# Transposed keys through DRAM in five transfers, with a new order of work, in a gated linear attention and PReLU network kernel

## The chip, the cores and the metric

The kernel runs on one core of a Trainium2 chip. The metric is the time of one execution on the device, in microseconds; the smaller the better. The profile comes from one execution of its own, and its times are counted from that execution's first instruction.

## The reference

Two blocks follow each other. The first is a recurrence over 768 positions with a state of 48 x 48 for each of 4 batches x 8 heads; the second is a network over all 3072 tokens with a PReLU between two matrices.

```python
f = 1.0 / (1.0 + np.exp(-f_logit))
for t in range(S):                      # S = 768
    state = f[:, :, t, :, None] * state + np.einsum('bhd,bhe->bhde', k[:, :, t], v[:, :, t])
    y[:, :, t] = np.einsum('bhd,bhde->bhe', q[:, :, t], state)
x = y.transpose(0, 2, 1, 3).reshape(B * S, H * D)     # 3072 x 384
h = x @ w_in                                          # 384 x 2048
g = np.maximum(h, 0.0) + alpha * np.minimum(h, 0.0)
return g @ w_out                                      # 2048 x 384
```

Everything is float32.

## The kernel before

**Steps.** The positions are cut into six chunks of 128 and the four batches into two pairs. One step handles one chunk of one pair, so there are 12 steps, numbered 0 to 11, alternating between the pairs. Steps 0 and 1 (`opening`) have no state to carry in; steps 2 to 11 are the "usual" ones (`usual`, L427). The recurrence of a step is turned into matrix products: scores inside the chunk (`raw`, `qu`, `off`), the part that comes from the carried state, and the new state. The tokens that come out go through the network (`network`, L812) while the next steps' recurrence is under way, so TensorE works on the network of step n-1 and the recurrence of step n at once.

**An order written out by hand.** The text `ORDER_WORDS` (L41) is a list of 1186 words. A word such as `5K` names part `K` of step 5, and the kernel issues the parts in the order of the list. For TensorE (PE), VectorE (DVE) and ScalarE (ACT) that is the order in which they execute. GpSimd (POOL) and SyncE (SP), which issue transfers, get their order from the framework's own scheduling. Words that the prediction names: `e` loads q, k, the gates f and v of a step; `f` is the sigmoid and copies, `F`, `g`, `G`, `h`, `i`, `l` the elementwise work on keys and queries; `k` the transposition of the keys on VectorE; `K` their way to where the matmuls can use them; `d` the state increments on TensorE; `D` and `M` add these to the state; `r`, `u`, `o` are score matmuls, `R`, `U`, `O` and `A` put their results into the score matrix A; `y` is the output product, `Y` and `X` its way to the network. In the network (`N`), `a` is a product with `w_in` into one bank, `r` and `c` the PReLU, `b` the third pass of a product taken in three passes (four of the eight parts, from step 3 on), `p` a block product with `w_out` (tiles `pa` to `pf`), `m`, `u`, `v`, `w` sums of blocks of the gated values (L881), `Y` and `Z` accumulating transfers issued by GpSimd. `I` and `J` are matmuls without a use that keep TensorE running at the start.

**The keys.** The state increment of a step is keys transposed times values. In a usual step, `fifth` (L465, word `k`) lets VectorE transpose the tile `ks` in blocks of 32 x 32 into `x["kt"]`; that tile is the buffer into which the gates were loaded (tag `f`, one buffer, L311). After that the blocks stand on the wrong partitions. `keys` (L469, word `K`) moves them with 16 transfers on SyncE's queue, from SBUF to SBUF: for each of four groups of 32 source partitions and each of four groups of 32 target partitions one transfer of 32 partitions x 8 runs of 32 or 16 floats (128 or 64 bytes), into the tile `ksn`. `increments` (L531, word `d`) then runs 64 small matmuls that read `ksn` and the values `vs`, into the tile `pd` (L540). As `f` has one buffer, the load of the next step's gates (L313, GpSimd's queue) can't start until the transfers have read `kt`.

**Other transfers on SyncE's queue** are the stores of the result (`store`, L764, tile `o`) and the way of the step's output tokens through DRAM (`given`, L497: two transfers to DRAM, L504, and one back, L506).

Of the kernel before, what the change touches and what calls it, by code (L numbers as in the profile page):

```python
# [8 lines left out]
F32 = mybir.dt.float32  # L9
# [37 lines left out]
0Np4 Y3 0Np5 1Y1 2G 1X W0 W1 W2 0Np6 W3 W4 W5 0Np7 1Na0 0No0 2h 1M 0No1 2i 1Na3 1Nr0 1Na1 Y4 Y5 2p 1Na2 1Nr1 3e 2q
Y6 1Na4 1Nr2 2k 2r0 2u0 2l W6 1Nc0 1Nr3 1Nc1 2K 1Nm0 1Nr4 1Nc2 2t W7 1Na5 1Nc3 1Nm1 1Nc4 1Na6 1Nr5 2R0 2r1 2U0 1Nr6
1Na7 Z3 2R1 2A0 1Nc6 2u1 1Nr7 1Nc5 2o Z4 1Np0 2U1 2O 1Nc7 2A1 2d 1Nk 1Np1 2D 3f 3F 2y0 2y1 2M 2Y0 2Y1 1Np2 1Np3 2X
1Nu0 3g 1Nu1 1Nv0 1Np4 1Nd 1Nv1 1Nw0 1Ng 3G 1Nw1 1Ne 1Nj 1Nh 1Np5 1Np6 3h 1Nf 1Nl 1Ni 3p 1Ns1 2Na2 2Na0 3i 1NL 1Ns0  # L50
2Nr0 2Na1 3l 2Nr1 4e 2Na3 3q 2Nr2 2Nc0 3r0 3u0 2Nr3 3k 2Nc1 3R0 2Nm0 3K 2Nc2 3t 2Na5 3U0 2Nc3 2Nm1 2Na4 2Nr4 3r1
2Nr5 3o 3R1 3A0 2Na6 2Nc5 3u1 2Nr6 2Nc4 2Nc6 3O 3U1 Z5 2Na7 3A1 3d 2Np0 3D 2Nr7 2Nk 2Np1 2Nc7 3y0 Z6 4f 2Nd T 3y1 4F
2Np2 3M 3Y0 3Y1 2Np3 2Nu1 2Nu0 4G 2Np4 2Nv0 4g 3X 2Nv1 2Ng 2Nw0 3Nx 3Ny 2Nw1 2Ne 2Nj 2Nh 2Np5 3Na0 3NY 4h 2Np6 2Nf
2Nl 4p 3Nz 4i 4l 2NL 4q 3Nr0 3Na2 2Ni 3Na1 4k 3Nr1 3Na7 3Na3 3Nr2 3Nc0 3Nc2 4t 3Nc1 4r0 3Nr7 3Nm0 4K 4u0 3Nc7 4R0
4U0 3Na5 3Na4 4r1 3Nq4 4u1 3NZ 3Nq3 2Ns1 4A0 2Ns0 3Nq5 3Na6 4R1 3Nq6 3Nb3 4U1 4o 4O 3Nr3 4d 3Nc3 4A1 3Nm1 3Nb6 3Nb4
5e 3Nb5 3Nr4 3Nr5 3Np0 4D 3Nr6 3Nc6 3Nc5 4y0 3Nc4 4y1 5f 4M 4Y0 4Y1 3Np2 3Nk 3Np1 5F 4X 3Np3 3Nu0 5g 3Nu1 3Nv0 3Nv1
3Ng 3Nw0 3Np4 4Nx 5G 4Ny 3Nw1 4NY 3Nd 3Ne 5h 3Nj 3Nh 3Np5 4Na2 5p 3Nl 4Nz 3Np6 3Nf 3Ni 4Na0 5i 5l 3NL 5q 4Nr0 4Na1
5k 4Nr1 4Nc0 4Nr2 5r0 5u0 4Nc1 4Nm0 5K 4Na3 4NZ 4Nc2 5t 5R0 5U0 4Na4 4Na7 4Nr7 4Nq3 3Ns1 4Nc7 6e 4Na5 5A0 5r1 4Nq4
5u1 3Ns0 4Nq5 5R1 5U1 4Na6 5o 4Nq6 4Nb3 5d 5O 4Nr3 5A1 4Nc3 4Nb5 4Nm1 4Nb6 5D 4Nb4 4Nr4 4Nr5 4Np0 4Nr6 5y0 4Nc4 4Nc5
6f 4Nc6 5y1 4Np2 5M 5Y0 5Y1 4Nk 4Np1 5X 6F 4Np3 4Nu0 6g 4Nu1 4Nv0 4Nv1 4Ng 4Nw0 5Nx 6G 4Np4 5Ny 4Nw1 5NY 4Nd 4Ne 6h  # L60
4Nj 4Nh 4Np5 5Nz 6p 4Nf 4Nl 4Ni 4Np6 5Na0 6i 6l 4NL 6q 5Nr0 5Na1 6k 5Na7 5Nr1 5Na2 5Nc1 6u0 5Nr2 5Nc0 6r0 5Nm0 6K
5Nc2 6t 6R0 5Na3 5Nr7 6U0 5Nc7 7e 5Na5 5Na4 6r1 5Nq4 5Nq3 4Ns1 6A0 6u1 5NZ 6R1 6U1 4Ns0 5Nq5 5Na6 5Nq6 5Nb3 5Nb4 6o
5Nr3 5Nc3 6O 6A1 6d 5Nb5 5Nm1 5Nb6 6D 5Nr4 5Nr5 5Np0 5Nr6 5Nc4 5Nc6 6y0 7f 5Nc5 7F 6y1 7G 5Nk 5Np1 5Np2 6M 6Y0 6Y1
6X 5Np3 5Nu0 7g 5Nu1 5Nv0 5Nv1 5Nw1 5Np4 6Nx 6Ny 5Ng 5Nw0 6NY 5Nd 5Ne 7h 5Nj 5Nh 5Np5 7p 5Np6 5Nf 5Nl 5Ni 7i 6Na0 7l
5NL 7q 6Nz 6Nr0 6Na1 6Na2 6Nr1 6Nc1 6Nr2 6Na3 6Nc0 7k 6Na7 6Nm0 7K 7r0 7u0 6Nc2 7t 7R0 6Nr7 7U0 6Nq3 5Ns1 8e 6Na5
6Na4 7A0 6Nq4 7u1 6NZ 7r1 6Nc7 5Ns0 6Nq5 7R1 7U1 6Na6 6Nq6 6Nb3 6Nr3 6Nc3 6Nm1 6Nb4 6Nb6 6Nb5 7o 6Nr4 6Nr5 6Nc4 6Nr6
7A1 7d 6Np0 6Nc5 7O 7D 6Nk 6Np1 7y0 8f 6Nc6 8F 7y1 7M 7Y0 7Y1 7X 8g 7Nx 6Np2 6Np3 7Nz 6Nu0 6Nu1 8G 6Np4 6Nv0 6Nd
6Nv1 6Ng 6Nw0 7Ny 7NY 6Nj 6Nw1 6Ne 6Nh 6Np5 8h 7Na0 6Nf 6Nl 8p 6Ni 6Np6 8i 8l 7Na1 7Na2 6NL 6Ns1 8q 7Nr0 8k 7Na7
7Nr1 8r0 7Nr2 8u0 7Nc0 7Nc1 7Nm0 8K 7Nc2 8t 9e 7Nr7 8R0 7Na4 7Na3 7Nq3 7Na5 8U0 7Nq4 8r1 8u1 7NZ 7Nc7 6Ns0 8A0 7Nq5
7Na6 8R1 8U1 7Nb4 7Nq6 7Nb3 7Nr3 7Nc3 7Nm1 7Nb6 7Nb5 8o 8A1 8d 7Nr4 7Nr5 7Nc4 7Nr6 8D 8O 7Np0 7Nc5 9f 7Nk 7Np1 7Nc6  # L70
8y0 7Nd 9F 8y1 8M 8Y0 7Np2 9r0 8Y1 8X 9g 7Ne 7Np3 7Nu0 7Nu1 9G 8Nx 7Np4 7Nv1 8Ny 7Nv0 7Ng 7Nw0 8NY 7Nw1 7Np5 7Nj 7Nh
# [29 lines left out]
def kernel(  # L101
# [62 lines left out]
    dram = ctx.enter_context(tc.tile_pool(name="dram", bufs=1, space=bass.MemoryType.DRAM))  # L164
# [262 lines left out]
    def usual(bp, c, x):  # L427

        i = f"{bp}_{c}"
# [38 lines left out]

        def keys():  # L469
            ksn = x["ksn"] = work.tile([128, U, HP * 128], F32, tag="ksn", name=f"ksn_{i}", bufs=1)  # L470
            for a in range(4):
                n = min(32, D - 32 * (a % 2))
                for b in range(NJ):
                    nc.sync.dma_start(  # L474
                        out=ksn[32 * b:32 * (b + 1)].rearrange("p u (h x) -> p (u h) x", h=HP)[:, :, 32 * a:32 * a + n],
                        in_=x["kt"][32 * a:32 * (a + 1)].rearrange("p (g b x) -> p g b x", b=NJ, x=32)[:, :, b, 0:n])
# [31 lines left out]
        def later():  # L508
# [507 lines left out]
```

## Time and profile before

| | |
|---|---|
| median of three executions | 605.23 us (604.7 to 606.34) |
| the profiled execution | 603.32 us |
| its span, first to last instruction | 601.5 us |
| TensorE busy / VectorE busy / ScalarE busy | 583.0 / 506.3 / 302.6 us |
| mean granted TensorE clock | 0.991 |
| key transfers (L474) | 160, of 32 or 16 KB |
| key transpositions (L467) | 10, of 1.245 us each |
| state increments (`pd`, L540) | 768 matmuls, 17.2 us busy |
| transfers through q1 (issued by SyncE) | 60224 packets, 30.61 MB |

In the views of the profile, L540 is line 540 of the kernel; "PEld" is TensorE's loading of weights, "SPq" or "PEldq" the instruction queue of an engine, where issues of transfers and semaphore instructions appear. A row of a wait reads: the waiting instruction, what released it, total us, number of waits, the longest. A row of the chain or of a timeline reads: start, length, engine, tile or line, number of instructions.

### The profile page before, as it was taken

Reading aid. Unit: us, or ns where it says so; the run is one execution under the profiler, and the core shown is the slowest. Engines: PE = TensorE matmul, PEld = TensorE weight load, DVE = VectorE, ACT = ScalarE, POOL = GpSimd, SP = SyncE. Lnnn points to the kernel's source line nnn. Section 1 sums busy time; section 2 is a strip of 40 time slices with the busy share of each in tenths; the row PEclk is TensorE's granted clock in tenths of the full one; section 3 lists DMA queues with packets and bytes.
Section 4 is the critical chain, followed back from the end, with each engine's and each line's share of the span. In section 5 each row is a group of like instructions: output and inputs, shape, how many; then the busy total and the mean of one; then the engine's idle time right before and its main releaser. Section 6 shows DMA issues by size and latency. Waiting matters only on the chain.

```text
span 601.5 us, 19099 instructions
## 1 busy us (share of the span) xinstructions
PE 583.0 (97%) x8200; PEld 529.5 (88%) x8200; DVE 506.3 (84%) x1027; ACT 302.6 (50%) x561; POOL 68.4 (11%) x114
## 2 busy tenths in 40 slices
PE   8699999999999999999999999999999999999997
PEld 6588768898889899999988889999899999899997
DVE  7889998999899889989979879989988979975333
ACT  5797963551472662563472374365366255452230
POOL 9210010000011011011011001101101100100100
PEclk9799999999999999999999999999999999999999
DMA  9959023320344343344334333533532423411300
GB/s 300 352 173 384 31 54 84 78 81 26 65 125 92 77 127 90 75 127 93 73 106 95 83 87 89 116 88 90 114 90 82 117 40 108 89 22 28 79 2 27
DMA packets 69925, 61.05 MB, mean 101 GB/s; under 512 B 46448, under 2 KB 60400, under 8 KB 69840
## 3 DMA queue, kind: packets, MB, share of 16 engines
q1 hardware_dynamic: 60224, 30.61, 18.7%
q0 software_dynamic: 8880, 28.84, 18.1%
q8 instruction: 65, 1.06, 0.8%
q10 hardware_dynamic: 736, 0.37, 0.2%
q14 instruction: 20, 0.16, 0.1%
HBM read 39.75 MB, written 8.26 MB: 80 GB/s over the span
## 4 chain that ended last, share of the span: by engine, by line
PE 70%; DVE 12%; SPq 7%; ACT 5%; DMA 4%; issue 2%; POOLq 0%; DVEq 0%; ACTq 0%
PE ph L832 30%; SPq L474 7%; PE pa L887 7%; PE pe L887 4%; PE pf L887 4%; PE pb L887 4%; PE pc L887 4%; PE pd L887 4%; PE py L615 3%; PE qu L592 2%; PE raw L583 2%; DMA f<-in_fT 2%; PE pd L540 2%; DVE gate L881 2%; PE po L867 2%
## 5 line engine op out<-in xcount | busy, mean ns | idle before, releaser
L832 PE MATMUL ph<-xT,w_in_sb 128*128 128x256 f32 x612 | 137.0, 380 | 0.0
L855 ACT ACTIVATE gate<-ph 128x512 f32<-128x512 f32 x96 | 55.4, 596 | 149.1 <-PE ph L832 131.3
L832 PEld LDWEIGHTS ph<-xT,w_in_sb 128*128 128x128 f32 x612 | 115.2, 190 | 15.8 <-issue 0.3
L860 DVE SCALAR_TENSOR_TENSOR gate<-gate,om,ph 128x256 f32<-128x256 f32 x192 | 80.7, 473 | 25.3 <-ACT gate L855 25.1
L887 PE MATMUL pa<-w_out_sb,gate 128*128 128x192 f32 x352 | 61.6, 328 | 0.0
L881 DVE TENSOR_TENSOR gate<-gate 128x512 f32<-128x512 f32 x88 | 57.1, 688 | 3.7 <-PE pb L887 3.0
L887 PEld LDWEIGHTS pa<-w_out_sb,gate 128*128 128x128 f32 x352 | 57.1, 190 | 0.5
L600 DVE COPY_PREDICATED ad<-mraw,raw 128x256 f32<-128x256 int32 (+1 forms) x96 | 42.8, 446 | 8.4 <-PE raw L583 5.9
L451 DVE COPY_PREDICATED ad<-mquad,qu 128x224 f32<-128x224 int32 (+6 forms) x140 | 42.2, 301 | 5.9 <-PE qu L592 0.5
L607 ACT COPY A<-ad 32x256 f32<-32x256 f32 x96 | 38.7, 403 | 14.8 <-DVE ad L451 13.3
L440 DVE TENSOR_TENSOR scores<-scores,fs 128x768 f32<-128x768 f32 (+5 forms) x60 | 37.3, 621 | 1.4
L832 PE MATMUL ph<-xh,hi 128*128 128x256 f32 x216 | 34.1, 294 | 0.0
L845 ACT ACTIVATE ph<-ph 128x512 f32<-128x512 f32 x36 | 20.1, 576 | 26.1 <-PE ph L832 10.9
L887 PE MATMUL pd<-t,gate 128*128 128x192 f32 x176 | 30.8, 328 | 1.9 <-DVE gate L881 1.9
L338 DVE TENSOR_TENSOR qd<-qd,f 128x768 f32<-128x768 f32 (+2 forms) x36 | 27.3, 758 | 5.4 <-ACT qd L331 5.4
L832 PE MATMUL ph<-xl,lo 128*128 128x256 f32 x216 | 31.7, 283 | 0.0
L887 PEld LDWEIGHTS pd<-t,gate 128*128 128x128 f32 x176 | 28.7, 190 | 3.0 <-DVE gate L881 3.0
L887 PE MATMUL pe<-w_out_sb,gate 128*128 128x192 f32 x176 | 30.7, 328 | 0.5 <-DVE o L897 0.5
L887 PE MATMUL pb<-t,gate 128*128 128x192 f32 x176 | 31.1, 330 | 0.0
L887 PE MATMUL pc<-t,gate 128*128 128x192 f32 x176 | 30.8, 328 | 0.0
L832 PEld LDWEIGHTS ph<-xh,hi 128*128 128x128 f32 x216 | 28.6, 190 | 2.4 <-issue 1.7
L365 ACT COPY scores<-qd 128x256 f32<-128x256 f32 x48 | 28.0, 686 | 5.1 <-DVE qd L338 5.0
(153 smaller groups left out, 1036.7 us busy)
## 6 DMA issues: line engine op xcount, KB each, us to landing
w_out_raw<-in_w_out SPq DMA_DIRECT2D x8, 767.8 KB, 10.5
w_in_raw<-in_w_in SPq DMA_DIRECT2D x8, 767.2 KB, 8.8
q<-in_qT POOLq DMA_DIRECT2D x11, 512.0 KB, 4.4
f<-in_fT POOLq DMA_DIRECT2D x11, 512.0 KB, 4.7
k<-in_kT POOLq DMA_DIRECT2D x11, 512.0 KB, 5.4
out<-o SPq DMA_DIRECT2D x24, 192.0 KB, 1.9
vs<-in_v POOLq DMA_DIRECT2D x22, 192.0 KB, 3.2
tokens<-y SPq DMA_DIRECT2D x18, 192.0 KB, 3.2
```

Of the source, the lines that this page charges most:

```text
L338: nc.vector.tensor_tensor(qdv[d], qdv[d - 1][:, :, :, 1:5 - d], f[:, :, 1:5 - d].rearrange("p (g i) r -> p g i r", i=NB), ALU.mult)
L365: nc.scalar.copy(x["q4"][:, :, :, r], qdv[r][:, :, :, 0])
L440: nc.vector.tensor_tensor(by_four(us[:, :, UO[m]:UO[m] + 4 * n]), by_four(us[:, :, skip:skip + 4 * n]), spread(fq[:, :, 1:1 + n], n), ALU. ...
L451: nc.vector.copy_predicated(ad[:, u, :, :, 4 * m:DB], mquad[:, lo:lo + n].bitcast(I32).unsqueeze(1).unsqueeze(1).broadcast_to((128, 2, HP, ...
L474: nc.sync.dma_start(out=ksn[32 * b:32 * (b + 1)].rearrange("p u (h x) -> p (u h) x", h=HP)[:, :, 32 * a:32 * a + n], in_=x["kt"][32 * a:32 ...
L600: nc.vector.copy_predicated(adu[:, :, :, d:4], mraw[:, d, :, d:4].bitcast(I32).unsqueeze(1).broadcast_to((128, H, NB, n)), rv[:, :, QO[d]: ...
L607: nc.scalar.copy(A[s_, u, :, s_], ad[s_, u].rearrange("p r h t -> p (r h) t"))
L832: nc.tensor.matmul(banks[f][:, j * T:(j + 1) * T], lhsT=of[:, kt, 128 * j:128 * (j + 1)], rhs=by[:, kt], start=first_ and kt + j == 0, sto ...
L855: nc.scalar.activation(to, of, AF.Relu, scale=-1.0)
L860: nc.vector.scalar_tensor_tensor(to[:, j], to[:, j], om[:, m:m + 1], of[:, j], ALU.mult, ALU.add)
L881: nc.vector.tensor_tensor(block(to)[:, p], block(x_)[:, p], block(y_)[:, p], op)
L887: nc.tensor.matmul(banks[to][:, 0:DH], lhsT=block(of)[:, f], rhs=of_w_out(by)[:, f], start=start and f == 0, stop=f == NH - 1, skip_group_ ...
```

## The change

`keys` of the usual steps gets a DRAM tile `turned` of 128 x 1024 floats (two buffers). Four transfers, one for each group of 32 source partitions, write `kt` into it in runs of 32 floats (all 32, where the old transfers left out 16 of the padding); a fifth reads it back into `ksn` in whole rows. The fifth reads what the four wrote, so it is issued after they have landed. Steps 0 and 1 transpose their keys on TensorE and are not touched by this.

```diff
         def keys():
             ksn = x["ksn"] = work.tile([128, U, HP * 128], F32, tag="ksn", name=f"ksn_{i}", bufs=1)
+            way = dram.tile([128, W], F32, tag="turned", name=f"turned_{i}", bufs=2)
             for a in range(4):
-                n = min(32, D - 32 * (a % 2))
-                for b in range(NJ):
-                    nc.sync.dma_start(
-                        out=ksn[32 * b:32 * (b + 1)].rearrange("p u (h x) -> p (u h) x", h=HP)[:, :, 32 * a:32 * a + n],
-                        in_=x["kt"][32 * a:32 * (a + 1)].rearrange("p (g b x) -> p g b x", b=NJ, x=32)[:, :, b, 0:n])
+                nc.sync.dma_start(out=way.rearrange("(b p) (g s) -> p g b s", b=NJ, s=128)[:, :, :, 32 * a:32 * (a + 1)],
+                                  in_=x["kt"][32 * a:32 * (a + 1)].rearrange("p (g b x) -> p g b x", b=NJ, x=32))
+            nc.sync.dma_start(out=ksn.rearrange("p u n -> p (u n)"), in_=way)
```

The text `ORDER_WORDS` is replaced as a whole. It has the same 1186 words in another order, from the first line to the last. Its beginning, and the stretch around the keys of step 5, before and after:

```diff
-0e 0I0 0f 0F 0g 0G 0h 0i 0m 0r0 0p 0j 0l 0r1 0q 0I1 0I2 0I3 0I4 0R0 a0 0I5 a1 0o 0O 1e a2 0s 0k 0J0 0K0 0u0 w0 0K1
+0e 1e 0I0 0f 0F 0G 0g 0h 0i 0m 0p 0j 0r0 a0 0r1 0I1 0l 0I2 0R0 0I3 0I4 0I5 a1 0q 0o 0O 0k a2 0s 0t 0K0 w0 0u0 0U0
...
-5k 4Nr1 4Nc0 4Nr2 5r0 5u0 4Nc1 4Nm0 5K 4Na3 4NZ 4Nc2 5t 5R0 5U0 4Na4 4Na7 4Nr7 4Nq3 3Ns1 4Nc7 6e 4Na5 5A0 5r1 4Nq4
-5u1 3Ns0 4Nq5 5R1 5U1 4Na6 5o 4Nq6 4Nb3 5d 5O 4Nr3 5A1 4Nc3 4Nb5 4Nm1 4Nb6 5D 4Nb4 4Nr4 4Nr5 4Np0 4Nr6 5y0 4Nc4 4Nc5
+4Nz 4Nq5 4Na1 5q 5t 4Nr1 4Nc0 4Nr2 5r0 5u0 4Nc1 4Nm0 5K 4Nc2 5R0 4NZ 4Na3 5U0 4Na7 4Nr7 4Na4 5r1 5A0 4Nq3 4Nq4 5u1
+4Nc7 5R1 5U1 4Na6 4Nb4 6e 4Nb3 5o 4Nq6 4Nr3 5d 5O 4Nc3 5A1 4Nm1 5D 4Nb6 4Nb5 4Nr4 4Nr5 4Np0 4Nr6 5y0 3Ns0 4Nc4 4Nc5
```

More of the change, by code (lines that the diff above doesn't have):

```diff
@@ L47 @@
[L47 to L56, printed above, removed]
@@ L62 @@
[L62 to L71, printed above, removed]
@@ new lines @@
+3A0 4e 2Nc5 3u1 2Nr6 2Nc4 3O 3U1 1Ns1 Z5 2Na7 2Nc6 Z6 3A1 3d 3D 1Ns0 2Np0 2Nr7 2Np1 2Nk 2Nc7 4f 2Nd 3y0 T 3y1 4F 3M
+3Y0 3Y1 2Np2 2Np3 2Nu1 2Nu0 4G 2Np4 3X 2Nv0 4g 2Nv1 2Nw0 2Ng 3Nx 3Ny 2Nw1 2Ne 2Nj 2Nh 2Np5 4h 2Np6 2Nf 4p 2Nl 2Ni
+3Na0 4i 3Nr0 2NL 3Na2 3NY 4k 4l 4q 2Ns1 3Nz 3Na1 4t 3Nr1 3Na7 3Na4 3Nr2 3Nc0 4K 3Nc2 3Nc1 4r0 3Nr7 3Nm0 4u0 3Nc7
+3Na6 3NZ 2Ns0 4R0 3Na3 4U0 4r1 3Na5 4u1 3Nq3 3Nq4 4A0 3Nq5 4R1 4U1 3Nq6 4o 4O 5e 3Nb3 3Nr3 3Nc3 3Nb4 3Nm1 3Nb6 3Nb5
+4d 3Nr4 3Nr5 3Np0 4D 4A1 3Nr6 3Nc6 3Nc5 4y0 3Nc4 4y1 5f 4M 4Y0 4Y1 3Np2 3Np1 3Nk 5F 4X 3Np3 3Nu0 5g 3Nu1 3Nv0 3Nv1
@@ new lines @@
+5Nz 5NZ 5Na5 6K 5Nc2 5Na4 6R0 5Nr7 5Na3 6U0 5Nc7 6r1 5Nq3 6A0 6u1 6R1 6U1 5Nq4 7e 5Nb3 5Nq5 4Ns0 5Na6 5Nb4 6o 5Nr3
+5Nq6 5Nc3 6O 6A1 6d 5Nm1 5Nb6 5Nb5 6D 5Nr4 5Nr5 5Np0 5Nr6 5Nc4 5Nc6 7f 6y0 5Nc5 7F 6y1 5Nk 7g 6Y0 6Y1 5Np2 5Np1 6X
+6M 5Np3 5Nu0 5Ng 5Nu1 5Nv0 5Nv1 5Nw1 7G 5Np4 6Nx 6Ny 5Nw0 5Nd 5Ne 7h 5Nj 5Nh 5Np5 5Np6 5Nf 7p 5Nl 5Ni 5Ns1 6Nz 6NY
+6Na0 7i 7l 6Nr0 6Na1 5NL 6Na2 7k 7q 6Nr1 6Nc1 6Nr2 6Nc0 6Na7 6Na3 6Nm0 7r0 7K 6Nc2 7u0 7R0 6Nr7 6NZ 7t 7U0 7A0 6Na5
+6Na4 6Nq4 7u1 6Nq3 6Nc7 7r1 6Nq5 6Na6 7R1 5Ns0 7U1 6Nq6 8e 6Nb3 6Nr3 6Nc3 6Nb4 6Nm1 6Nb6 6Nb5 7o 6Nr4 6Nr5 7A1 7O
@@ new lines @@
+9r0 9p 7Nl 7Ni 7Ns1 8Nz 8NY 8Na0 8Na7 9i 8Nr0 8Na1 7NL 8Na2 9k 8Na5 9l 9q 9u0 9t 8Nr1 8Nr2 8Nc0 8Na3 9R0 8Nc2 8Nc1
+9K 8Nr7 8Na4 8NZ 8Nm0 9U0 8Nq4 9A0 8Nq3 8Nq5 9r1 9u1 8Na6 8Nc7 9R1 9U1 8Nq6 10e 8Nb3 8Nb4 8Nr3 8Nc3 8Nm1 8Nb6 8Nb5
+8Nr5 9o 7Ns0 8Nr4 8Nc5 9A1 8Nr6 9O 9d 8Np0 8Nc4 9D 8Nk 8Np1 8Nc6 10f 9y0 9y1 8Np2 10F 9Y0 9Y1 10g 9X 9M 8Np3 8Nu0
+8Nu1 10G 8Np4 9Nx 8Nd 10r0 8Nv0 8Nv1 8Nw0 8Ng 8Np5 8Ne 8Nw1 10h 9Ny 8Nh 8Nj 8Np6 8Nf 10p 8Nl 8Ni 9Nz 9NY 9Na0 9Nr0
+8NL 10i 9Na1 9Na2 10k 10l 9Na7 10q 10t 9Nr1 9Nr2 9Nc0 9NZ 9Nc2 9Nc1 10K 9Nr7 10R0 8Ns1 9Na3 9Nm0 9Nc7 9Na4 10u0 10U0
@@ new lines @@
+10Nr5 10Np0 11d 11U1 10Nr6 10Nc5 11o 10Nc6 11A1 10Nc4 11O 11D 10Nk 10Np1 10Np2 10Nd 10Nu0 11y0 10Nu1 11y1 11Y0 10Nv0
+10Nv1 11Y1 11M 11X 10Np3 10Nw0 10Ng 10Ne 10Nw1 10Np4 10Np5 10Nj 11Nx 10Nh 11Ny 11Na7 10Nf 10Nl 10Ni 11Nz 11NY 11Na0
+10Np6 11Nr0 11Na1 10NL 11Na2 11Nc0 11Na3 10Ns1 11Nr1 11Nc1 11Nm0 11Nr2 11Na4 11NZ 11Nc2 11Nr7 11Na5 11Nq3 11Nq4
+10Ns0 11Na6 11Nq5 11Nb3 11Nc7 11Nq6 11Nb4 11Nr3 11Nb5 11Nc3 11Nr4 11Nr5 11Nm1 11Nb6 11Np0 11Nc4 11Nr6 11Nc5 11Nc6
+11Nk 11Np1 11Np2 11Nd 11Np3 11Nu0 11Nu1 11Nv0 11Nv1 11Np4 11Nw0 11Ng 11Ne 11Nw1 11Np5 11Nj 11Nh 11Nl 11Np6 11Nf 11Ni
@@ L88 @@
+11NL 11Ns1 11Ns0
 """
```

45 lines of the change are left out of this document (22 added, 23 removed).

## The prediction

> **What bounds the kernel now.** I read the page's busy times first, then the busy time in stretches of 20 us, the chain of waits, the waits by engine, and last each step's state increments (tile `pd`, line 540), which read the transposed keys.
>
> ```profile
> PE 583.0 (97%) x8200; PEld 529.5 (88%) x8200; DVE 506.3 (84%) x1027; ACT 302.6 (50%) x561; POOL 68.4 (11%) x114
> PE   8699999999999999999999999999999999999997
> PE ph L832 30%; SPq L474 7%; PE pa L887 7%; PE pe L887 4%; PE pf L887 4%; PE pb L887 4%; PE pc L887 4%; PE pd L887 4%; PE py L615 3%; PE qu L592 2%; PE raw L583 2%; DMA f<-in_fT 2%; PE pd L540 2%; DVE gate L881 2%; PE po L867 2%
> ksn<-f SPq DMA_DIRECT2D x80, 32.0 KB, 2.8
> ksn<-f SPq DMA_DIRECT2D x80, 16.0 KB, 2.5
> POOL f L313 <- DMA ksn<-f: 46.4, 4, 15.5
> PE pd L540 <- DMA ksn<-f: 2.1, 4, 1.2
> ```
>
> TensorE is busy 583.0 of 601.5 us. By the stretches, 7.9 us of its idle time lie before 40 us, 6.85 us between 60 and 540, 2.2 us after that. So an edit to the usual steps can win only idle time, or busy time that is not work. The chain names the second: 7% of it is SyncE issuing the 160 key transfers of line 474, which no other engine's row would show.
>
> One step, from the chain and the timeline (start, length, what):
>
> ```profile
> 195.32 1.26 DVE f L467
> 208.56 2.40 DMA ksn<-f
> 211.05 0.89 PE pd L540 x57
> 353.64 1.61 PE L540 MATMUL pd<-vs,ksn 64*48 64x48 f32 x64
> L540 PEldq EVENT_SEMAPHORE  x9: 51/51/51, 353.3 to 354.3; - x9
> 164.52 0.94 PE L540 MATMUL pd<-vs,ksn 64*48 64x48 f32 x64
> L540 PEldq EVENT_SEMAPHORE  x2: 51/51/51, 164.1 to 164.3; - x2
> ```
>
> The transposition ends at 196.58, sixteen issues run from 196.63 to 208.5, the last transfer lands at 210.96: 14.4 us from transposed keys to usable keys. The same 64 matmuls take 0.94 us where two semaphore instructions stand before them (step 3), and 1.61 us where nine are spread among them (step 7) and nothing is late. Sixteen transfers mean many semaphores; TensorE pays for them inside its busy time.
>
> **The change part by part.**
>
> *The waits at pd (removed).* Length of the pd group with the idle time in and before it, steps 4 to 11: 3.02, 2.17, 2.79, 1.61, 1.65, 1.67, 1.65, 1.58. Less 0.94 each, the excess is 2.08 + 1.23 + 1.85 + 0.67 + 0.71 + 0.73 + 0.71 + 0.64 = 8.6 us. Steps 4 to 6 are late data as well, steps 7 to 11 waits alone. Afterwards one transfer fills `ksn`, so one wait is left: a semaphore instruction of 51 ns and about as much around it, 0.1 x 8 = 0.8. Gain **7.8 us**, if the data is there in time.
>
> *The way of the keys (changed).* Before: 16 issues of 0.61 us and 0.04 between, two of them longer by about 1.0 (1.54 and 1.80 in step 4), and 2.4 to landing. After: four transfers to DRAM, each of 32 partitions x 8 x 4 runs of 128 B, 1024 runs; SyncE waits for all four, then issues one transfer of 128 rows of 4 KB. The number of short runs stays 4096 a step, 256 on each of 16 engines. What one costs is not in the trace. From below: in the stretch 96.0 to 109.4 the queue held 24.6% of 16 engines for 4352 packets, 13.4 x 16 x 0.246 / 4352 = 12 ns, SBUF to SBUF, mostly 64 and 128 B. From above: the token transfers to DRAM, 126.6 to 130.2, 32.4% for 416 packets of mostly 1 KB, 45 ns. A line through both gives about 14 ns at 128 B, which I take, the size being nearest to the lower row; 256 x 14 = 3.6 us (ends 3.1 and 11.5). Four issues of the old 0.61 take 2.6 us and lie beside that; if an issue grew with its runs, four would take what sixteen take now, 9.8, which lies inside the upper end. Landing adds 2.0 (stores of `o`: 1.9). So the four have landed 0.6 + 3.6 + 2.0 = 6.2 us after the first issue (5.7 to 14.1). Read-back: 0.1 for the wait, then 3.4 from issue to landing, from the token read-back (384 KB, 3.0 in the step at 130.6) and 128 KB more at its 390 GB/s. Keys usable after 9.7 us (9.2 to 17.6) instead of 14.4; with the transposition's 1.25, 11.0.
>
> The Trainium skill, in DMA: Bandwidth & Descriptors, section Specifications, speaks against this: below 512 B an engine reads, modifies and writes, so 128 B runs miss line rate. No run here shows such runs into DRAM; read as a doubling, 14 ns becomes 28 and the keys come 3.6 us later, which is the slow rival below.
>
> *Is 11.0 covered?* I added up the TensorE work standing between words k and d of a step in the new order: a whole part 12 x 0.224 = 2.69 (three-pass parts 1.83 and 0.80), a block product 2.65, raw 0.86, qu 0.9, off 0.8, py 1.0. Steps 2 to 11: 10.6, 10.6, 20.2, 18.6, 18.6, 17.5, 17.5, 14.0, 19.3, 19.4. The old order: 15.0, 13.3, 15.1, 15.1, 18.6, 15.7, 17.5, 16.7, 16.6, 20.2; its trace has 25, 16.0, 14.1, 14.2, 14.5, 15.8, 14.9, 15.2, 18.3, 19.6 from transposition to pd, so the text is good to some 3 us, and VectorE ran ahead in steps 2 and 3. Those two are the only ones near 11.0: cost 0, up to 0.4 each.
>
> *Next load.* The transposed keys lie in the buffer of the gates `f`, so GpSimd's load of the next `f` waited for the key transfers (46.4 us in four waits) and then took 4.5 to 5 us before the sigmoid. It becomes free after 6.2 us instead of 14.4. This start of VectorE's chain feeds the idle time elsewhere, 6.85 less pd's own 3.2 (its waits after 60 us: 2.1 for the transfers, 0.5, 0.4, 0.2), 3.6 us. I take half, **1.8** (ends 0 and 3.6): other rows of it wait for VectorE's gate sums.
>
> *New wait on SyncE.* The fifth transfer holds the queue some 5 us. Behind it stand stores of `o`, for which nobody waits soon, and the tokens, issued 24 to 31 us after the first key transfer (96.2 and 126.8; 196.6 and 220.4). Cost 0; without that distance, up to 5 us in a step. Extra traffic is 1 MB a step where engines stand at 20 to 49%: nothing.
>
> *New order.* Same 1186 words, same work per engine. Before the first big matmul (41.1 us) TensorE's sequence is nearly the same; the move of step 1's load words to the front changes little, since `q` waited for the `qd` copy of step 0. One spot got tighter: step 4's A1 has 1.0 us of TensorE work before y1 (6.0 before) and its copies take 4 x 0.41 = 1.65. For that and others unseen I put **+2.0** (ends -1 and +5).
>
> Sum: -7.8 - 1.8 + 2.0 = **-7.6 us**. The profiled execution took 603.32 (span 601.5), 1.9 under the median of three, 605.23 (604.7 to 606.34); I expect 595.7 for such a profile and **597.6** for the median.
>
> **Rivals.**
>
> *Nothing to measure:* TensorE gets its 8 us and gives them back, waiting for VectorE, which is busy 89.9% between 60 and 540 us (431.5 of 480); idle time moves from pd to pa..pf. For it: pd L887 waits 1.9 us for gate sums already. Against: VectorE has 48 us of idle time there and its load comes earlier. About 604.5.
>
> *Slower:* the short runs into DRAM are dear. At t ns a run the keys need 7.4 + 0.256 t us from the transposition's start. Steps with 10.6, 10.6, 14.0 break first. At 28 ns: 14.6, late by 4.0 + 4.0 + 0.6 = 8.6, the gain is gone and the change is about +1; that is the deciding point. At 35 ns, 16.4: 5.8 + 5.8 + 2.4 = 14.0, 611; at 45 ns, 18.9: 8.3 + 8.3 + 0.3 x 2 + 1.4 x 2 + 4.9 = 24.9, 622. For it: the DRAM row is 45 ns. Against: it carries eight times the bytes. By the skill's rule, taken as that doubling, the time is about 606.
>
> *The order alone:* idle time elsewhere grows by 5 instead of 2, 600.6; still faster.
>
> **How the numbers follow.** A measurement here tells about 0.3% (1.8 us) from no change. Forecast and its milder kin (592 to 603.4): 0.68. Nothing to measure, with the slow case at its deciding point: 0.12. Slower: 0.20. The low end is everything won, 605.2 - 8.6 - 3.6 - 1 = 592.0. Upward the range reaches 608, which takes in 30 ns a run (keys after 15.1, late by 4.5 + 4.5 + 1.1, 607.7) and leaves out some 0.15. The forecast's own range is 593 to 602.
>
> **What would show it.** Right: pd at 0.9 to 1.1 us in every step with one or two semaphore instructions; L474's rows gone and two new ones, the read-back landing 9 to 11 us after the first issue; `f` loads issued some 8 us nearer to the transposition; SyncE out of the chain; idle time between 60 and 540 us at 2 to 5. Wrong: pd waiting 2 us or more for the read-back in steps 2, 3 and 9 (slow runs); write issues above 2 us each; or pd short and TensorE's idle time as large as before at gate, y or b parts (VectorE or the order).

## The result, and the profile after

| | before | after |
|---|---|---|
| median of the runs | 605.42 us (604.7 to 606.34, 4 runs) | 597.65 us (596.98 to 601.4, 4 runs) |
| ratio, 95% interval | | 0.9884 (0.984 to 0.9927) |
| the profiled execution | 603.32 us | 601.4 us |
| its span | 601.5 us | 599.6 us |
| TensorE busy | 583.0 us | 582.6 us |
| TensorE idle between 60 and 540 us | 6.84 us | 6.98 us |

The change is worth 7.8 us. The profiled execution of after is the longest of its four runs. Three more profiles of the same kernel come from the experiments below; their spans are 593.8, 597.3 and 596.5 us.

The page of the kernel after: busy times, the chain of waits by engine and by line, and two rows of transfers (KB each, median us from issue to landing).

```profile
PE 582.6 (97%) x8200; PEld 530.7 (89%) x8200; DVE 506.5 (84%) x1027; ACT 301.9 (50%) x561; POOL 68.5 (11%) x114
...
PE 83%; DVE 8%; ACT 6%; issue 2%; DMA 1%; ACTq 0%; DVEq 0%
PE ph L831 39%; PE pa L886 7%; PE pe L886 5%; PE pf L886 5%; PE pd L886 4%; PE qu L591 4%; PE pc L886 3%; PE pb L886 3%; PE raw L582 3%; PE po L866 3%; PE py L614 3%; DVE qd L338 2%; ACT A L606 2%; PE pd L539 1%; DVE ad L451 1%
...
turned<-f SPq DMA_DIRECT2D x40, 128.0 KB, 4.8
ksn<-turned SPq DMA_DIRECT2D x10, 512.0 KB, 3.8
```

SyncE's 7% have left the chain. The 160 key transfers are 40 writes and 10 read-backs.

Step 4, from the timelines of SyncE, VectorE, GpSimd and TensorE of the kernel after (start, length, what; in brackets the idle time before it and what ended that):

```profile
191.89 1.25 DVE L467 STREAM_TRANSPOSE f<-ks 128x1024 f32<-128x1024 f32 x1
193.16 4.70 SPq L473 DMA_DIRECT2D turned<-f  x4
202.39 0.34 SPq L475 DMA_DIRECT2D ksn<-turned  x1
202.93 0.75 POOL L313 DMA_DIRECT2D f<-in_fT  x1 [6.83 <-DMA turned<-f]
209.13 0.70 PE L566 MATMUL off<-q,kh 48*32 48x32 f32 x58 [0.97 <-issue]
212.81 0.94 PE L539 MATMUL pd<-vs,ksn 64*48 64x48 f32 x64
```

The four writes start at 193.16; SyncE has waited for all of them by 202.39, 9.2 us later. With 3.8 for the read-back the keys are usable at some 206.2, and `pd` needs them at 212.81. It runs in 0.94 us, as in every step of this profile (0.93 or 0.94 ten times; before, with the idle time in and before it, 1.61 to 3.02 in steps 4 to 11). The gates' load is issued 9.8 us after the first key transfer (before: 196.63 and 211.80, 15.2).

One line has no counterpart before. TensorE stands still for 0.97 us in the middle of the `off` matmuls and nothing in the profile releases it ("issue"). I call this a stop, and count those of 0.3 us and more. The rows of TensorE's waits in the kernel after (total us, number, longest):

```profile
PE ph L831 <- issue: 2.2, 1, 2.2
...
PE qu L591 <- issue: 1.4, 1, 1.4
...
PE off L566 <- issue: 1.0, 1, 1.0
```

That is 4.6 us of the 7 us of idle time between 60 and 540. Before had one such stop of 0.48 us and 2.1 us of `pd` waiting for `ksn`. And a stop may cost more than its length. TensorE by stretches of 4 us (stretch, its length, busy us and matmuls, granted clock, share of the DMA engines, GB/s), kernel after:

```profile
250.00:254.00 4.00, 2.57 (x131) 1.00 0.89 269
254.00:258.00 4.00, 4.00 (x41) 0.57 0.32 124
258.00:262.00 4.00, 4.00 (x149) 1.00 0.02 6
```

Behind the stop of 1.43 us the clock is at 0.57 for a stretch: 41 matmuls run where there was room for more, and this counts as busy. The 0.57 is a mean; a narrower stretch shows 0.50 for 3.4 us:

```profile
254.20:257.60 3.40, 3.40 (x22) 0.50 0.36 142
```

A second dip, 0.50 from 349.77 to 353.18, follows the stop of 2.19 us. The three other profiles of this kernel have the stops at the same instructions, and one more inside `pd` of step 5 (0.44 to 0.84 us), but between 60 and 540 us their clock stays at 1.00.

### The profile page after: what moved, and what is told of

Same layout as the page of the kernel before. It is cut to its first block, busy times and chain, and to the rows that moved or that the text cites. A ratio compares the mean times of both kernels' runs of the same rounds, so it can differ in the third digit from the quotient of the medians.

```text
span 599.6 us, 18858 instructions
## 1 busy us (share of the span) xinstructions
PE 582.6 (97%) x8200; PEld 530.7 (89%) x8200; DVE 506.5 (84%) x1027; ACT 301.9 (50%) x561; POOL 68.5 (11%) x114
## 3 DMA queue, kind: packets, MB, share of 16 engines
q1 hardware_dynamic: 59744, 37.16, 22.0%
q8 instruction: 64, 1.05, 0.7%
## 4 chain that ended last, share of the span: by engine, by line
PE 83%; DVE 8%; ACT 6%; issue 2%; DMA 1%; ACTq 0%; DVEq 0%
PE ph L831 39%; PE pa L886 7%; PE pe L886 5%; PE pf L886 5%; PE pd L886 4%; PE qu L591 4%; PE pc L886 3%; PE pb L886 3%; PE raw L582 3%; PE po L866 3%; PE py L614 3%; DVE qd L338 2%; ACT A L606 2%; PE pd L539 1%; DVE ad L451 1%
## 5 line engine op out<-in xcount | busy, mean ns | idle before, releaser
L854 ACT ACTIVATE gate<-ph 128x512 f32<-128x512 f32 x96 | 55.0, 595 | 121.2 <-PE ph L831 107.6
L831 PE MATMUL ph<-xh,hi 128*128 128x256 f32 x216 | 35.3, 300 | 0.0
L424 ACT COPY A<-q 48x512 f32<-48x512 f32 x44 | 27.1, 617 | 15.2 <-DVE q L398 14.8
L831 PEld LDWEIGHTS ph<-xl,lo 128*128 128x128 f32 x216 | 29.3, 197 | 2.4 <-issue 2.4
L323 POOL DMA_DIRECT2D vs<-in_v x22 | 13.2, 605 | 154.6 <-PE py L614 154.4
```

The costliest lines, as they stand in the source:

```text
L424: nc.scalar.copy(A[halves(cc)[1], :, par * HP:(par + 1) * HP, CH * cc:CH * (cc + 1)], x["q3"][rows(par)].rearrange("p (u h c) s t -> p u h ...
L831: nc.tensor.matmul(banks[f][:, j * T:(j + 1) * T], lhsT=of[:, kt, 128 * j:128 * (j + 1)], rhs=by[:, kt], start=first_ and kt + j == 0, sto ...
L854: nc.scalar.activation(to, of, AF.Relu, scale=-1.0)
```

## The experiments

Times are medians; the ratio is to the kernel before, run on the same chip at the same time, with its 95% interval. Runs with the same first letter ran side by side.

| run | us | ratio |
|---|---|---|
| `e0_after_again` | 597.56 | 0.991 (0.9878 to 0.9942) |
| `e1_way_alone` | 597.51 | 0.9894 (0.9869 to 0.9918) |
| `e2_order_alone` | 599.24 | 0.9922 (0.9896 to 0.9947) |
| `e3_readback_in_eight` | 600.13 | 0.994 (0.9918 to 0.9962) |
| `f0_after_yardstick` | 598.21 | 0.9869 (0.9848 to 0.989) |
| `f1_rows_in_eight` | 603.87 | 0.9966 (0.9943 to 0.999) |
| `f2_spare_traffic` | 603.27 | 0.9947 (0.9922 to 0.9973) |
| `f3_rows_out_runs_back` | 604.33 | 0.9982 (0.9966 to 0.9998) |
| `g0_after_third_yardstick` | 597.86 | 0.9882 (0.9855 to 0.991) |
| `g1_long_runs` | 605.21 | 1.0012 (0.9991 to 1.0033) |
| `g2_long_runs_sixteen` | 606.03 | 1.0031 (1.0013 to 1.005) |
| `h1_late_load` | 595.66 | 0.9853 (0.9825 to 0.9881) |

Before's median was 604.61 (e), 606.19 (f), 604.62 (g) and 604.6 (h). Single runs of one kernel spread by about 1%.

### The change taken apart: the way alone, the order alone

The kernel after once more, as a yardstick:

> The changed kernel as it is, as the yardstick for the next runs. 597 to 598 us by every theory. If its TensorE stops of 1.4 and 2.2 us inside a group of equal matmuls (at 252 and 347 us of the first profile) belong to its order or its transfers, they come back at the same places; if they are chance, they are gone or elsewhere.

Then the new way of the keys with the old text of the order, and the old sixteen transfers with the new text:

```diff
 # the way alone: keys() as after, the text as before
-ORDER_WORDS = (new text)
+ORDER_WORDS = (old text)
 # the order alone: keys() as before, the text as after
-ORDER_WORDS = (old text)
+ORDER_WORDS = (new text)
```

> Five transfers through DRAM with the old order. Theory W (the waits at pd are the gain): every pd group near 0.94 us, late data at steps 4 to 6 less by the 1 to 2 us that the keys come earlier, so 598 to 601 us. Theory O (the new order is the gain, the way of the keys only shifts): 604 to 606 us.

> Sixteen transfers from SBUF to SBUF with the new order. Theory W: pd groups stay at 1.6 us with nine semaphore instructions, only the late data of steps 4 to 6 (about 3 us) goes, steps 2 and 3 may wait for keys (10.6 us of cover against 15.7): 602 to 605 us. Theory O: 597 to 599 us.

Way alone: -7.1 us. Order alone: -5.4. Both: -7.05. They don't add. (Without its one execution at 604.86 us the median of the way alone is 597.29.) The lengths of the `pd` groups say why. I add up, for each profile, what its ten groups (idle time in and before them included) take over 0.94 us each: before 8.8 us, order alone 4.6, way alone 2.2, both 0.9. The old order with sixteen transfers was late by up to 2 us in steps 4 to 6; the new order puts more work before `pd` there and cures that, and the way through DRAM cures the same steps and the semaphores besides. What the order leaves, two rows of the order alone show: the 64 matmuls of step 7 on TensorE's timeline, and the semaphore instructions in its queue.

```profile
349.50 1.58 PE L540 MATMUL pd<-vs,ksn 64*48 64x48 f32 x64
L540 PEldq EVENT_SEMAPHORE  x9: 51/51/51, 349.1 to 350.1; - x9
```

Nothing is late in that step, nine semaphore instructions stand in it, and it takes 0.64 us more than 0.94. The kernel after has one there:

```profile
L539 PEld LDWEIGHTS pd<-vs,ksn x64: 116/122/122, 355.3 to 356.0; 64*48 64x48 f32 x64
L539 PEldq EVENT_SEMAPHORE  x1: 51/51/51, 355.1 to 355.1; - x1
```

It also matters where the semaphore instructions stand. In step 4 of the order alone there are eight of them, all ahead of the group, and `pd` takes 0.94 us; in step 7 above they run until 350.1, among the matmuls that start at 349.50.

```profile
212.09 0.94 PE L540 MATMUL pd<-vs,ksn 64*48 64x48 f32 x64
L540 PEldq EVENT_SEMAPHORE  x8: 51/51/875, 210.0 to 211.7; - x8
```

### Is it the number of transfers or the waits? The read-back in eight

```diff
-            nc.sync.dma_start(out=ksn.rearrange("p u n -> p (u n)"), in_=way)
+            for part in range(8):
+                cols = slice(128 * part, 128 * (part + 1))
+                nc.sync.dma_start(out=ksn.rearrange("p u n -> p (u n)")[:, cols], in_=way[:, cols])
```

> The changed kernel with its read-back cut into eight transfers of 512 B rows: the same bytes, but eight semaphores for pd instead of one. Theory W: the pd groups go from 0.94 to about 1.6 us, times ten steps, 603 to 605 us. Theory O: at most 1 us more than the changed kernel, since the order still covers the keys: 598 to 599 us.

The matmuls take their groups of columns in order, so eight transfers by columns are eight possible waits. But in the six steps in which the data was in time `pd` took 0.94 us, and step 7 shows one semaphore instruction: the number of transfers by itself costs nothing. In the other four it took 1.83 to 2.9 us: the eight issues take 5 us in place of 0.33, so the keys come later, and steps 2 and 3 wait (1.83 and 2.3); two stops fall into `pd` of steps 5 and 7 (1.12 and 1.76 us). So the loss of 2.6 us against the yardstick measures late keys and stops, not what it was made to measure.

So a cut that needs more waits was tried, four groups of rows by two halves of the columns:

```diff
-            nc.sync.dma_start(out=ksn.rearrange("p u n -> p (u n)"), in_=way)
+            for b in range(NJ):
+                for u in range(U):
+                    rows_, cols = slice(32 * b, 32 * (b + 1)), slice(512 * u, 512 * (u + 1))
+                    nc.sync.dma_start(out=ksn.rearrange("p u n -> p (u n)")[rows_, cols], in_=way[rows_, cols])
```

> The changed kernel as it is, the yardstick beside the next three. Median 597 to 598 us; TensorE stops without a visible cause some 2 us in the profile, at the places seen so far (inside groups of equal matmuls near 208, 251 and 345 us).

> The read-back again in eight transfers, but cut by rows and pairs of batches, so that one matmul of pd reads two of them; when it was cut by columns, each matmul read one, no semaphore instruction was added (20 before pd as with one transfer) and the pd groups stayed at 0.94 us where the data was in time. Theory W (what stretches pd is a semaphore instruction between matmuls): at least four more semaphore instructions a step and pd groups of 1.2 to 1.6 us, 1 to 3 us over the cut by columns (600.1), so 601 to 603. Theory N (the number of transfers or their late landing stretches pd): the same pd groups and the same time as the cut by columns.

Here five semaphore instructions stand in a step. In time, `pd` takes 1.05 us, 0.11 more; steps 3 and 5, where the keys are late, take 2.63 and 3.08. The row of TensorE's waits that names this:

```profile
PE pd L542 <- DMA ksn<-turned: 3.2, 3, 1.9
```

TensorE waits 3.2 us for late keys. The `pd` groups take 5.6 us over 0.94 in all, the yardstick's 0.7, and this is most of the 5.7 us between the two kernels; the stops are alike (4.3 and 4.5 us). Five semaphore instructions in place of one cost 0.11 us, nine cost 0.64 to 0.7, and eight ahead of the group cost nothing: not a fixed price for each. What else than their place it depends on was not separated.

### More traffic that nobody waits for

The kernel does all its work and, in every usual step, copies the 512 KB of `turned` into a second DRAM tile that nobody reads:

```diff
             nc.sync.dma_start(out=ksn.rearrange("p u n -> p (u n)"), in_=way)
+            spare = dram.tile([128, W], F32, tag="spare", name=f"spare_{i}", bufs=2)
+            nc.sync.dma_start(out=spare, in_=way)
```

> The changed kernel with one more transfer a usual step, DRAM to DRAM, 512 KB, issued right behind the read-back; nobody waits for it. Theory F (the stops without a visible cause are TensorE waiting for its own instructions, whose loads stand behind the data on the same 16 engines): the stops grow from about 2 to 5 us or more in total, at the same instructions, and the time goes to 600 to 606 us. Theory C (they are chance, or belong to the clock): unchanged, 597 to 599 us, since no instruction waits for the spare bytes.

It is 5.1 us slower than its yardstick, and the intervals of the ratios are clear of each other. `pd` takes 0.94 us in nine steps and 2.53 in step 5, 1.38 of that a stop. Up to step 6 the two profiles run together (`pd` at 304.6, the yardstick's at 304.1). Then comes a stop of 2.76 us before 350.15, and this, TensorE by stretches in the kernel with spare traffic (columns as above):

```profile
344.00:348.00 4.00, 3.40 (x141) 1.00 0.74 256
348.00:352.00 4.00, 1.84 (x8) 0.68 0.38 137
352.00:356.00 4.00, 4.00 (x21) 0.50 0.00 0
```

The yardstick has a stop of 1.61 us at that instruction and the clock at 1.00 in all three. In step 7 `pd` starts at 357.3, the yardstick's at 353.0. The clock is at 0.50 from 349.4 to 356.2. So traffic is not free: it comes back as a longer stop and 6.8 us at half clock. That it does so through the stops is read from one profile of each kernel.

### The short runs on the other side of DRAM

One write in rows of 4 KB, four read-backs in runs of 128 B:

```diff
-            for a in range(4):
-                nc.sync.dma_start(out=way.rearrange("(b p) (g s) -> p g b s", b=NJ, s=128)[:, :, :, 32 * a:32 * (a + 1)],
-                                  in_=x["kt"][32 * a:32 * (a + 1)].rearrange("p (g b x) -> p g b x", b=NJ, x=32))
-            nc.sync.dma_start(out=ksn.rearrange("p u n -> p (u n)"), in_=way)
+            nc.sync.dma_start(out=way, in_=x["kt"])
+            for b in range(NJ):
+                nc.sync.dma_start(out=ksn[32 * b:32 * (b + 1)].rearrange("p u (h a x) -> p (u h) a x", a=4, x=32),
+                                  in_=way.rearrange("(a p) (g b x) -> p g a b x", a=4, b=NJ, x=32)[:, :, :, b])
```

> The way through DRAM mirrored: one transfer writes the transposed keys in whole rows of 4 KB, four read them back in runs of 128 B. If short runs are dear as writes into DRAM alone, keys come 3 us or more earlier than with the changed kernel's 12 to 13 us and the next load of the gates starts 5 us earlier; time 596 to 598 us. If a short run costs the same either way, keys come at about the same time, and the earlier load changes little: 597 to 599 us, with four transfers to wait for at pd costing up to 0.3 us a step.

```profile
turned<-f SPq DMA_DIRECT2D x10, 512.0 KB, 3.8
ksn<-turned SPq DMA_DIRECT2D x40, 128.0 KB, 6.4
```

The same short runs land after 6.4 us as reads from DRAM and after 4.8 as writes to it. That is not the price of a run alone: the load of the next gates starts when the write has landed, so it runs beside the reads. In step 11, where no such load follows, the reads land after 4.0 us. The kernel loses 6.1 us against its yardstick. `pd` tells 1.0 of that (1.7 over 0.94 in all, against 0.7), and the stops outside `pd` 1.4 (5.4 us against 4.1). The remaining 3.7 us these two sums don't show. Some 2.3 of them lie in the choice of the profiled execution: the two profiled executions are only 3.8 us apart (602.94 and 599.13).

### Fewer and longer runs

The transposition writes its result in another order, so that a partition's 256 floats for one target group lie together. The runs become 1 KB, and the state increments read weights with a stride:

```diff
-            nc.vector.transpose(x["kt"], x["ks"].rearrange("p g s t -> p (g s t)"))
+            nc.vector.transpose(x["kt"].rearrange("p (b t g) -> p b g t", b=NJ, t=DB),
+                                x["ks"].rearrange("p (g c) s t -> p (c s) g t", c=NC2))
...
-                                         lhsT=ksn[s_, u, hp * 128 + 64 * par:hp * 128 + 64 * par + D],
+                                         lhsT=ksn[s_, par, 0:D, u * HP + hp] if c else
+                                         ksn[s_, u, hp * 128 + 64 * par:hp * 128 + 64 * par + D],
```

A second kernel has the same layout, but sixteen transfers from SBUF to SBUF in place of the way through DRAM.

> The changed kernel as it is, the yardstick beside the next two: 597 to 598 us, TensorE stops without a visible cause of 2 to 4.5 us in the profile.

> The changed kernel with the transposed keys laid out so that what goes to one row of the DRAM tile from one group of partitions is one run of 1 KB in place of eight of 128 B: 512 runs a step, not 4096. Theory F (stops come from full transfer engines): four writes landed 4 to 5 us after the first issue in place of 7.7 to 9.6, the next gates' load 4 us earlier, the engines' busy time for the writes down from 256 x 14 ns to 32 x 45 ns each, stops down to 1 us or less in total: 594 to 596 us. Theory C (stops are chance; the keys are covered anyway): the keys come earlier, nobody needs them, 597 to 598 us. A slower transposition or slower weight loads of pd (strided) would show in their rows as more than 1.25 us and more than 0.94 us a step.

> The same layout, but moved from SBUF to SBUF in sixteen transfers of 1 KB or 512 B runs, with the new order. Theory W (what is left at pd with sixteen transfers are semaphore instructions): pd groups again about 1.6 us in most steps, no stops without a visible cause, 597 to 599 us as with the order alone and short runs (599.2). If the groups shrink to about 0.94 us, the stretch came from transfers that landed late, not from their number, and the time is 594 to 596 us.

Long runs through DRAM: the writes land sooner and the queue has less to do.

```profile
q1 hardware_dynamic: 23904, 37.16, 19.3%
turned<-f SPq DMA_DIRECT2D x40, 128.0 KB, 3.2
L467 DVE STREAM_TRANSPOSE f<-ks x10: 2035/2046/2083, 104.2 to 519.5; 128x1024 f32<-128x1024 f32 x10
L540 PEld LDWEIGHTS pd<-vs,ksn x768: 116/186/194, 30.5 to 544.1; 64*48 64x48 f32 x192
```

Landing falls from 4.8 to 3.2 us and the packets of SyncE's queue from 59744 to 23904. It wins nothing, because the keys were in time already, and it pays: a strided weight load takes 186 ns in place of 122, so `pd` takes 1.68 us in place of 0.94, and the transposition 2.05 us in place of 1.25. Ten times 0.74 is 7.4 us, as much as the kernel lost against its yardstick (605.21 - 597.86 = 7.35). What the longer transposition adds, 0.8 us a step on VectorE, was not separated.

The pair shows the semaphores cleanly, with one order and one layout. Step 7 with sixteen transfers, then with five (timelines of TensorE):

```profile
355.54 2.34 PE L540 MATMUL pd<-vs,ksn 64*48 64x48 f32 x64
```

```profile
356.28 1.69 PE L540 MATMUL pd<-vs,ksn 64*48 64x48 f32 x64
```

Nine semaphore instructions stand in the first. In steps 7 to 10 `pd` takes 2.32 to 2.39 us with them and 1.68 to 1.69 without, 0.65 us a step with no data late.

### The gates' load held back

Many stops fall where GpSimd's loads of `f` and `k` hold most of the 16 engines while TensorE runs groups of small matmuls, 64 with 64 weight loads in 0.9 us: the engines are busy for 78 to 99% of the stop at `off` in the four profiles of after. Here one small transfer keeps the load of `f` until the read-back has landed:

```diff
             nc.sync.dma_start(out=ksn.rearrange("p u n -> p (u n)"), in_=way)
+            nc.sync.dma_start(out=ksn[0:1, 0, D:D + 4], in_=x["kt"][0:1, 0:4])
```

> The kernel after, and one transfer of 16 bytes more on SyncE's queue behind the read-back in each usual step: from the transposed keys into four padding columns of the key tile. It writes the tile that the read-back fills, so it leaves only when that has landed, and the next gates' load, which overwrites the transposed keys, has to wait for it. All work and its order stay; only the loads of f and k come later, by the 4 to 6 us of the read-back and the small transfer: f some 14 to 17 us after the first key transfer in place of 10 to 11. Theory 1 (TensorE's stops without a visible releaser, 2.2 to 5.3 us in the runs of this kernel, come where GpSimd's loads fill the 16 DMA engines while TensorE is in the groups of small matmuls): the loads now fall behind these groups, the stops shrink to under 1 us in all, pd stays at 0.94 to 1.05 in a step, and the time is 594.5 to 596.5, a ratio to the kernel before of 0.980 to 0.985. Theory 2 (the stops have another cause, or come by chance): the stops stay at 2 to 5 us and the time at 597 to 599, 0.987 to 0.991. Theory 3 (the early gates' load is what brings the gain, as the prediction's term of 1.8 us has it): the sigmoid and VectorE's chain wait for f again, idle time of TensorE at pa to pf grows by 2 us or more, and the time is 599 to 602, 0.991 to 0.996.

595.66 us, 2 us under the three medians of the kernel after, 597.56 to 598.21. The ratio's interval, 0.9825 to 0.9881, overlaps with that of each of the three, so this is a hint and no proof of a better kernel. From the rows of TensorE's waits (one of the two at `qu`, 0.8 us, lies before 60 us):

```profile
PE qu L592 <- issue: 2.5, 2, 1.7
...
PE pd L887 <- DVE gate L881: 1.0, 2, 0.7
PE ph L832 <- issue: 0.4, 1, 0.4
```

The next gates' load of step 4 is issued at 211.72, 17.4 us after the first key transfer (194.29), later than in before (15.2). Theory 3 falls: TensorE waits no longer for gate sums (1.0 us, as in after), and the time did not grow. With the new order the early load brought nothing that shows; with the old order no run holds it back. Theory 1 holds in part at most. The stops at `off` and in `pd` are gone and the rest is 2.1 us; the yardsticks have 2.2, 4.5 and 4.2, so one of them has no more. And a stop of 1.72 us is left at `qu`, before 254.21, and in it the engines stood nearly idle, as the DMA queues in just this stretch show (packets, MB, share):

```profile
q0 software_dynamic: 2, 0.01, 5.4%
q1 hardware_dynamic: 3, 0.01, 2.9%
q14 instruction: 1, 0.01, 1.5%
```

So full engines during a stop are not what makes it. The stops inside `pd` of the three yardsticks say the same: no packet of any queue starts in them.

What ends a stop the packet records of the traces do show. Queue q8 moves instructions in packets of 16 KB, 64 in the kernel after for TensorE's 8200 matmuls, 8200 weight loads and 166 others, so one for some 260 instructions. Before the stop of 1.43 us at `qu` (252.25 to 253.68) such a packet starts at 251.45, as the queues from 251.4 to 251.5 show:

```profile
q8 instruction: 1, 0.02, 59.3%
```

59.3% of 16 engines for 0.1 us is 0.95 us, so it has landed at 252.40, and TensorE goes on 1.28 us later. All 45 stops between 60 and 540 us in the 14 profiles end so, 1.2 to 1.6 us after a q8 packet has landed, though these packets come only every 9 us or so. The waits with a releaser end 0.1 to 17 us after one. By this timing TensorE waits for its own instructions in a stop. Among small matmuls 260 instructions are work for 1.8 us (128 take 0.9), so by this estimate they run out soonest there. Why the packet comes late is open: no row shows when it was asked for. That it queues behind data in the time before would fit, and no run here separates it.

### Two sums against twelve times

Before's `pd` over 0.94 (8.8) plus its stop (0.5) is 9.3 us. The same sum for each profile, and what 9.3 less that would save beside what was saved:

| kernel | `pd` over 0.94 | stops outside `pd`, 0.3 us and more | would save | saved |
|---|---|---|---|---|
| `e0`, `f0`, `g0` (after) | 0.9, 0.7, 1.1 | 1.5, 4.1, 3.4 | 6.8, 4.5, 4.8 | 7.1, 8.0, 6.8 |
| `e1` way alone | 2.2 | 4.1 | 3.0 | 7.1 |
| `e2` order alone | 4.6 | 0.3 | 4.4 | 5.4 |
| `e3` read-back in eight | 5.5 | 2.1 | 1.7 | 4.5 |
| `f1` rows in eight | 5.6 | 3.7 | 0.0 | 2.3 |
| `f2` spare traffic | 1.6 | 3.5 | 4.2 | 2.9 |
| `f3` rows out, runs back | 1.7 | 5.4 | 2.2 | 1.9 |
| `g1` long runs | 8.0 | 3.1 | -1.8 | -0.6 |
| `g2` long runs, sixteen | 11.9 | 0.7 | -3.3 | -1.4 |
| `h1` late load | 0.6 | 2.1 | 6.6 | 8.9 |

Saved less would-save is +1.7 us on average, between -1.3 (spare traffic) and +4.1 (way alone). Before's own profiled execution, 603.32, lay 1.3 to 2.9 us under the four medians of before, which is about that average. Both columns part the kernels in much the same way: after and the late load on top, the long runs at the bottom, the rest between. The way alone is the exception: it saved as much as after, and its sum says 3.0. So `pd` and the stops are most of what these kernels differ in. The rest is the difference between one profiled execution and a median of many, the stops and the clock behind them above all; the order among the middle ones the sums don't give.

## Why the prediction was right, and where it was not

The time was forecast at 597.6 and came at 597.65, and the mechanism is the one forecast. The sum behind it was -7.8 - 1.8 + 2.0; what the runs show in its place is about -8.1 at `pd`, nothing for the load, nothing for the order, and some 3 us of stops given back (2.9 more than before, over the four profiles of after). These make -5.2. The profiled executions themselves differ by 4.7 us (603.32, and 598.61 on average over the four of after), which fits; the rest of the 7.8 us is that before's profiled execution lies 2.1 us under the median of its runs and those of after 0.8 over theirs. The terms for the load and the order, -1.8 and +2.0, are wrong and cancel each other. That the total agrees to 0.1 us is luck.

**The waits at `pd` (-7.8): right.** 0.94 us in all ten steps of the profile after, 0.7 to 1.1 us over that in all in the other three, where a stop falls into `pd`. Over the four profiles of after this term is 8.1 us. The one wait that is left costs nothing over the 0.94, where 0.1 us was put down. That it is the waits and not late data the pair with long runs shows in steps 7 to 10: 0.65 us a step.

**The price of a short run into DRAM (14 ns): right.** In the kernel after, from first write to read-back of step 4, the DMA queues show

```profile
q0 software_dynamic: 288, 0.92, 40.7%
q1 hardware_dynamic: 4160, 0.52, 39.3%
```

so 9.3 us x 16 x 0.393 / 4160 = 14.1 ns a packet. The slow rival needed 28. The Trainium skill, DMA: Bandwidth & Descriptors, section Specifications, has runs under 512 B miss line rate, and that agrees: in the kernel with long runs a packet of 1 KB took 3.8 x 16 x 0.59 / 576 = 62 ns (291.7 to 295.5), 7.8 ns for 128 B. What doesn't follow is that DRAM makes it dearer than the old way: the 12 ns from SBUF to SBUF are a mean over runs of 64 and 128 B, and by the packet records those of 128 B took 13.5 ns on average before and 13.8 after. The prediction's reading of the rule as twice 14 was wrong.

**Landing of the writes (6.2 us): too short.** 7.7 to 9.6 us from first write to read-back. The row above gives a reason: GpSimd's load of `q` holds 40.7% of the engines in the same 9.3 us. The way alone has the case without it: in its step 11 no load is under way, and the writes have landed after 5.8 us (518.8 to 524.6, in which they hold 61.5% of the engines). So, as far as one step tells, the price of the runs was right and the sharing of the engines was left out. The four issues took 3.0 to 6.2 us in place of 2.6, single ones up to 3.4. The prediction names issues above 2 us as a sign of being wrong; here they cost TensorE no time, since the keys were covered even so. The read-back took 3.2 to 5.0 us, 3.8 in the median, in place of 3.4. So the keys were usable after 10.9 to 14.7 us, not 9.7.

**Cover (10.6 us in steps 2 and 3): too short as well.** From first write to `pd` it was 16.7 us in step 2 (104.52 to 121.2) and 14.4 in step 3 (151.24 to 165.67); counted from the transposition, as the 10.6 is, 18.0 and 15.7. The transposition came earlier than the text of the order has it. These two errors hid each other: with the landing as measured and the cover as read from the text, those steps would have waited for some 2 us each. The margin is small: a read-back that takes 5 us to issue made both steps late.

**The next load (-1.8): wrong.** The load did move by 5.4 us (8 forecast), and ScalarE's wait for it fell from 10.3 to 1.7 us. But the kernel with the load held back was no slower, and there this wait is 1.8 us, in the order alone 2.9: the new order shortens it without an earlier load. Nothing on TensorE waited for that load.

**The new order (+2.0): wrong.** On top of the new way it is worth nothing that these runs can tell (597.51 and 597.56). Alone it gains 5.4 us, by the same late steps that the way cures. The prediction did not weigh the order as a gain to be had without the way.

**SyncE and the new wait: right.** SyncE has left the chain. TensorE waits once for tokens, 0.3 us at 90 us, but the order alone has this wait too (0.36), so it is not the new wait that makes it.

**Extra traffic at nothing: wrong.** This is the step that failed most plainly. Idle time between 60 and 540 us was to be 2 to 5; it is 6.98, 4.47, 6.90 and 6.52 in the four profiles of after, since stops of 2.2 to 4.6 us have come in place of the waits. All kernels with the way through DRAM have stops of 2.1 to 6.0 us in all; before, the order alone, and sixteen transfers of long runs have 0.3 to 0.7. So the stops come with the way, not with the order and not with short runs (3.1 us with runs of 1 KB), by one profile of each kernel and four of after. 512 KB a step more cost 5.1 us. By the packet records the stops are waits for TensorE's own instructions; why these come late with the way is open. The dips of the clock come on top: 3.41 us at half clock lose 1.7 us of TensorE's time by an estimate from the rows, and after's own profile has two.

**Rivals.** "Nothing to measure" fell on the measurement, though its picture, idle time moved and not removed, is partly what the profile shows: the place was the stops and not VectorE's sums (1.0 us). "Slower" fell with its 28 ns. "The order alone", 5 us more of idle time elsewhere, fell too: in that run TensorE stands idle for 2.9 us between 60 and 540 in all.

## What to carry to other kernels

A group of small matmuls that needs many transfers pays for the semaphores even when all data is there, where they fall among its matmuls: 0.65 us a step for nine of them. Gather the data with one last transfer, if the detour is covered by other work, and check that cover by the trace and not by counting words. Two edits that cure the same wait don't add, so try each alone; here the order alone brought 5.4 of the 7 us without a byte of extra traffic.

## What the hardware showed that was not expected

TensorE stops for 0.3 to 3.1 us with no releaser in the profile, in each of the kernels that send the keys through DRAM, mostly at the same instructions in every run. Each ends 1.2 to 1.6 us after a packet of 16 KB of its instructions has landed. Full DMA engines at the time of the stop are common, but not needed.

Around the end of some stops the granted clock falls to 0.50 for 3.41 us: with stops of 1.43 and 2.19 us (after), 1.76 (read-back in eight), 3.06 (way alone) and 2.55 (rows in eight), and for 6.8 us with 2.76 (spare traffic). With stops of 1.44, 1.61, 1.72, 1.76 and 1.85 in other profiles it stays at 1.00. So the length of a stop alone does not decide.

The clock records of the traces show a grid. The two dips of after start at 254.20 and 349.77, 28 times 3.413 us apart, and in each of the 14 profiles all low stretches, those at the kernel's start and end included, start whole multiples of 3.413 us apart. Cut into windows on this grid, TensorE stood idle for 1.76 to 3.03 us of the window just before five of the six dips between 60 and 540 us. Every window with so much idle time is followed by a dip; the most idle time without one is 1.73 us. Before the sixth dip it was 1.43 us, and the rest of that window holds almost only small matmuls. So a stop that the grid cuts in two can pass: of the 1.76 us in the third yardstick 1.52 fell into one window. The Trainium skill, TensorE: Matmul & The Clock Gate, section Why this matters for your kernels, asks for no idle gap of more than about 3 us between bursts. These traces show that less is enough at times.

A weight load of 64 x 48 with a stride takes 186 ns in place of 122, and the transposition of 128 x 1024 with a strided result 2.05 us in place of 1.25. Transfers of 128 KB in runs of 128 B land after 6.4 us as reads from DRAM, with a load of 512 KB beside them, and after 4.8 as writes.
